# A fused attention, MoE and MLP kernel: the high and low parts of x moved together in the first product of all residual tiles, and the first units' rows gathered at once when planned

## The chip, the cores and the metric

The kernel runs on one core of a Trainium2 chip. The metric is the device time of one execution in microseconds (us), the median of the runs shown. The engines are TensorE (PE, matmuls; PEld is its weight load), VectorE (DVE), ScalarE (ACT), GpSimd (POOL, here mostly the issuer of gathers and scatters) and SyncE (SP, the issuer of the other transfers). Each engine takes its instructions in the order in which they stand in its own program and waits for the others by semaphores.

## The reference

```python
# attention without softmax: 8 sequences of 3072, d_qk 64, D 256
attn = np.maximum(z @ z.T / S, 0.0) ** 2
x = u * (attn @ v)                                   # 24576 rows of 256 in all
# top-1 mixture of 8 experts, 256 -> 1024 -> 256
expert_idx = argmax of (x/|x|) @ (emb/|emb|).T / tau ; gate_w = its softmax value
out[mask] = gate_w[mask, None] * (np.maximum(x[mask] @ w1[e], 0) @ w2[e])
# MLP, 256 -> 2048 -> 256, with g = ELU
y = ELU(out @ w_in) @ w_out
```

## The kernel before

**Number format.** Each float32 operand is split into a high part of type `fp32r`, which PE multiplies at full rate, and a low part, also `fp32r`, that holds the remainder. A product is three matmul passes: high by high, low weight by high operand, high weight by low operand. ACT usually makes the high part (a copy or a relu), DVE the low part (a subtraction).

**Steps.** The whole program is a list of steps, written out by Python. Step `n` issues in this order: its own `h` (a first product on PE into a score buffer `pss`, and the ACT work on it), then `d1` to `d4` of step `n - 1` (the work on DVE), prepared tasks (`pre`), the second product `acc` of step `n - 2` (into an accumulator `psa`), `g`, and the side tasks that a planner put at step `n` (splits of weights, transposes, loads, gathers). The order on each engine is the order in which this program calls it. There are two score buffers of 128x1024 float32 (`t_ps`), two accumulators (`t_acc`), 39 ordinary slots of 128x1024 float32 and five wide tiles of twice that.

**Stages.** 576 attention steps come first. While they run, rows of x are stored to memory (`xr`), routed to experts group by group, and their numbers are scattered by expert into a table (`tok`). Then come units:
- 41 A units: a tile of 512 tokens of one expert through `w1` and `w2`, four steps each (A0 to A3). Their result, x2 (split into `x2h` and `x2l`), goes into
- an M unit each: the MLP on the same 512 tokens, eight steps (M0 on), 12 score matmuls of 512 columns and 12 in the second product.
- 17 residual units for tokens that fill no tile of 512, two steps each (B0, B1): 14 of 256 tokens (B) and 3 of 128 tokens (N). Each stands between an A unit and its M unit. More of them sit behind a condition on the number of tiles (`rest_tiles`).
- 7 D units: the MLP on the residual tokens, scattered into dense rows before.

In a residual unit the operand x lies with its high and low parts side by side in one tile, `xb` (high first), and one step makes 512 hidden units: four groups of 128 (`fi`), each over two halves of D (`kc`). Its function before is `ab_h`, with `ab_d` for the low part.

**Rows of a unit.** `rows_ops` makes its instructions: four gathers of token numbers (`gi`), four gathers of rows of x with the gate value (`gx`), both on POOL; the gating on DVE (`gate`); the store of the gated rows (`put`, to `xg`) and their load in a transposing layout (`get`, to `xt`) on SP. The loop over `units` says at which step each is issued: `wr` for the gathers, `w` for the weights, `wp_` for gating and store. `n` is the unit's first step, and `p1` (541) the step at which the plan of the first six A units is ready; A0 of the first unit is step 576, that of the second 580.

Of the kernel before, what the change touches and what calls it, by code (L numbers as in the profile page):

```python
# [7 lines left out]
F32 = mybir.dt.float32  # L8
# [21 lines left out]
def attn_moe_mlp(ctx, tc, zT, zK, uT, v, emb, embT, tau, wp, w_in, w_out, out):  # L30
# [40 lines left out]
    fixed = {}  # L71
# [62 lines left out]
    def cp(o, a):  # L134
        act.activation(out=o, in_=a, func=AF.Copy)  # L135
# [910 lines left out]
    TOK = {"A": 4, "B": 2, "N": 1}  # L1046
    W1, W2, XT, IDS, WST, WI, WO, X2 = {}, {}, {}, {}, {}, {}, {}, {}
# [45 lines left out]
    def rows_ops(key):  # L1093
# [9 lines left out]
        def gi(t):  # L1103
            def fn():
                if t == 0:
                    IDS[key] = again("ids") if fixed else sb.tile([128, 4], I32, name="ids", tag="ids", bufs=8)
                    h["x"] = wide("rows", [4, XW])
                gather(IDS[key][:, t:t + 1], tok[:, :], idx(t), E * N - 1)
            return fn

        def gx(t):
            def fn():
                known = N - 6 * 512 if kind == "A" and j < NA1 else N
                gather(h["x"][:, t], xr[:known, :], IDS[key][:, t:t + 1], known - 1)
            return fn
# [3 lines left out]
        def gate(t):  # L1119
            def fn():  # L1120
                x = h["x"][:, t]
                ts(x[:, :D], x[:, :D], x[:, D:D + 1], ALU.mult)
            return fn

        def put():
            sp.dma_start(rows.rearrange("(t p) d -> p t d", p=128), h["x"][:, :nt, :D])
# [8 lines left out]
    def xt_ops(key, h, dst, nt):  # L1135
# [5 lines left out]
        def hi():  # L1141
            if nt == 4:
                dst[key] = rslot("xh"), rslot("xl")
            else:
                t = rslot("xb").rearrange("p a (b c) -> p a b c", b=2)[:, :, :, :nt * 128]
                dst[key] = t[:, 0], t[:, 1]
            cp(dst[key][0], h["f"])
# [5 lines left out]
    def ab_h(key, i):  # L1153
# [19 lines left out]
        HL[key, i] = [hi, None]  # L1173

# [408 lines left out]
    fns = {"A": {"h": ab_h, "d1": ab_d, "acc": a_acc}, "B": {"h": ab_h, "d1": ab_d, "acc": b_acc}, "M": mf, "D": mf}  # L1583
# [133 lines left out]
    for un in units:  # L1717
# [3 lines left out]
        if k in "ABN":  # L1721
# [5 lines left out]
            if un == units[0]:  # L1727
                w, wr = n - 16, n - 24
                assert wr >= lo_
# [3 lines left out]
            elif un == units[1]:  # L1733
                wr = n - 16
# [17 lines left out]
            wp_ = n - (16 if un == units[0] else 10) if early else max(wr + 3, n - 11)  # L1752
            at(wp_, lambda gates=gates, put=put: ([g_() for g_ in gates], put()))
            at(wp_ + (5 if un == units[0] else 3) if early else max(wr + 5, n - 9), get)
# [109 lines left out]
```

## Time and profile before

| what | value |
|---|---|
| device time, median of 3 runs | 5083.72 us (5082.21 to 5088.95) |
| profiled execution, device time | 5085.41 us |
| its span, first to last instruction | 5083.6 us |
| mean granted clock of PE | 0.999 |
| PE matmul, busy | 5065.6 us |
| DVE, busy | 4022.5 us |
| ACT, busy | 3429.4 us |
| POOL, busy | 1356.7 us |

The span is what the profile times; the device time holds some 2 us around it. Matmuls overlap in the profile: one of 512 columns is shown with some 0.39 us, though the next starts 0.23 us behind it, so the time of a row of matmuls is read from the start of the row to the start of the next.

### The profile page before, as it was taken

Reading aid. Unit: us, or ns where it says so; the run is one execution under the profiler, and the core shown is the slowest. Engines: PE = TensorE matmul, PEld = TensorE weight load, DVE = VectorE, ACT = ScalarE, POOL = GpSimd, SP = SyncE. Lnnn points to the kernel's source line nnn. Section 1 sums busy time; section 2 is a strip of 40 time slices with the busy share of each in tenths; the row PEclk is TensorE's granted clock in tenths of the full one; section 3 lists DMA queues with packets and bytes.
Section 4 is the critical chain, followed back from the end, with each engine's and each line's share of the span. In section 5 each row is a group of like instructions: output and inputs, shape, how many; then the busy total and the mean of one; then the engine's idle time right before and its main releaser. Section 6 shows DMA issues by size and latency. Waiting matters only on the chain. (4 is left out here: it accounts for less than half of the span.)

```text
span 5083.6 us, 66094 instructions
## 1 busy us (share of the span) xinstructions
PE 5065.6 (100%) x23324; PEld 4198.1 (83%) x23324; DVE 4022.5 (79%) x5281; ACT 3429.4 (67%) x4140; POOL 1356.7 (27%) x1147
## 2 busy tenths in 40 slices
PE   9999999999999999999999999999999999999999
PEld 7888888888888878888888888888888888888887
DVE  8787878788787877887877877877777777777887
ACT  8686767767676756676666666666666666666776
POOL 0011111101111134324443444443333333330011
PEclk9999999999999999999999999999999999999999
DMA  8797988887978784324333334333333333221221
GB/s 247 216 242 215 242 217 230 221 242 214 252 200 239 195 253 145 85 71 119 111 113 115 107 112 121 107 113 109 95 85 85 85 85 85 85 81 38 47 48 40
DMA packets 666978, 726.38 MB, mean 143 GB/s; under 512 B 407724, under 2 KB 509487, under 8 KB 651280
## 3 DMA queue, kind: packets, MB, share of 16 engines
q1 hardware_dynamic: 593648, 518.67, 38.7%
q0 software_dynamic: 72992, 203.42, 12.9%
q8 instruction: 186, 3.05, 0.3%
q14 instruction: 152, 1.25, 0.1%
HBM read 451.63 MB, written 258.33 MB: 140 GB/s over the span
## 5 line engine op out<-in xcount | busy, mean ns | idle before, releaser
L138 PE MATMUL psa<-hi,v 128*128 128x512 f32 x4608 | 1147.2, 391 | 3.6 <-ACT hi L135 2.2
L138 PEld LDWEIGHTS psa<-hi,v 128*128 128x128 f32 x4608 | 858.9, 188 | 189.4 <-issue 7.4
L138 PE MATMUL pss<-x2h,wi 128*128 128x512 f32 x2624 | 808.5, 389 | 0.0
L138 PE MATMUL psa<-hi,wo 128*128 128x512 f32 x3008 | 743.0, 389 | 0.0
L127 DVE SCALAR_TENSOR_TENSOR y<-e,y 128x1024 f32<-128x1024 f32 x385 | 467.5, 1214 | 269.6 <-ACT e L1378 255.3
L138 PEld LDWEIGHTS psa<-hi,wo 128*128 128x128 f32 x3008 | 564.5, 188 | 116.9
L1259 ACT ACTIVATE e<-pss 128x1024 f32<-128x1024 f32 x376 | 386.5, 1028 | 398.7 <-PE pss L138 382.3
L818 POOL DMA_INDIRECT tok<-idt,pi x192 | 234.8, 1223 | 1469.9 <-DMA tok<-idt,pi 807.7
L138 PE MATMUL psa<-lo,v 128*128 128x512 f32 x2304 | 616.9, 390 | 1.3 <-issue 1.3
L1055 POOL DMA_INDIRECT out<-o,ids x192 | 215.6, 1123 | 1479.6 <-DMA o<-orow 1020.1
L1171 ACT ACTIVATE hi<-pss 128x1024 fp32r<-128x1024 f32 (+1 forms) x198 | 201.1, 1016 | 566.8 <-PE pss L138 548.5
L138 PEld LDWEIGHTS pss<-x2h,wi 128*128 128x128 f32 x2624 | 490.4, 188 | 99.9
L441 ACT ACTIVATE r<-pss 128x1024 f32<-128x1024 f32 x289 | 296.1, 1025 | 373.4 <-PE pss L138 370.9
L138 PE MATMUL pss<-x2l,wi 128*128 128x512 f32 x1312 | 510.4, 389 | 0.0
L138 PEld LDWEIGHTS psa<-lo,v 128*128 128x128 f32 x2304 | 433.0, 188 | 92.6 <-issue 1.7
L117 DVE TENSOR_TENSOR y<-r,y 128x1024 f32<-128x1024 f32 x385 | 470.7, 1223 | 33.7 <-DVE y L127 0.9
L117 DVE TENSOR_TENSOR lo<-y,hi 128x1024 fp32r<-128x1024 f32 x385 | 470.9, 1223 | 22.9 <-issue 0.5
L117 DVE TENSOR_TENSOR lo<-r,hi 128x1024 fp32r<-128x1024 f32 x336 | 382.7, 1139 | 103.0 <-ACT hi L135 97.9
L1378 ACT ACTIVATE e<-e 128x1024 f32<-128x1024 f32 x383 | 406.8, 1062 | 12.1
L1377 ACT ACTIVATE y<-e 128x1024 f32<-128x1024 f32 x383 | 406.4, 1061 | 9.5
L138 PE MATMUL psa<-hi,w 128*128 128x512 f32 x1312 | 405.2, 390 | 0.0
L138 PE MATMUL pss<-xh,w 128*128 128x512 f32 x1312 | 404.1, 389 | 0.1
(197 smaller groups left out, 9015.8 us busy)
## 6 DMA issues: line engine op xcount, KB each, us to landing
mir<-mt SPq DMA_DIRECT2D x480, 256.0 KB
mw<-mir SPq DMA_DIRECT2D x120, 1024.0 KB
vs<-v SPq DMA_DIRECT2D x48, 512.0 KB
u<-uT SPq DMA_DIRECT2D x48, 512.0 KB
xr<-xt SPq DMA_DIRECT2D x192, 128.0 KB
x<-xr SPq DMA_DIRECT2D x96, 256.0 KB
orow<-xt SPq DMA_DIRECT2D x188, 128.0 KB
o<-orow SPq DMA_DIRECT2D x47, 512.0 KB
```

The source lines that it names most:

```text
L117: vec.tensor_tensor(out=o, in0=a, in1=b, op=op)
L127: vec.scalar_tensor_tensor(out=o, in0=a, scalar=s, in1=b, op0=op0, op1=op1)
L138: pe.matmul(o, lhsT=l, rhs=r, start=start, stop=stop, skip_group_check=True, tile_position=pos)
L441: act.activation(out=r, in_=p, func=AF.Relu, scale=1.0 / S)
L818: pool.indirect_dma_start(out=tok[:, :], out_offset=bass.IndirectOffsetOnAxis(ap=h["pi"][:, t:t + 1], axis=0), in_=K["idt"][:, gt:gt + 1], ...
L1055: pool.indirect_dma_start(out=dst, out_offset=bass.IndirectOffsetOnAxis(ap=idx, axis=0), in_=src, in_offset=None, bounds_check=bound, oob_ ...
L1171: act.activation(out=hi, in_=p, func=AF.Relu)
L1259: act.activation(out=e, in_=p, func=AF.Relu, scale=-1.0)
L1377: act.activation(out=y, in_=e, func=AF.Tanh, scale=0.5)
L1378: act.activation(out=e, in_=e, func=AF.Exp, scale=-1.0)
```

## The change

Three things change.

1. Residual units get functions of their own, `b_h` and `b_d`. For each group and half of D, one matmul moves high and low part of x together against the high weights (512 columns for B, 256 for N), and a second moves the high part against the low weights (256 or 128) into the high part's columns. A score therefore takes twice the columns: a B step fills two score buffers, an N step one. ACT copies the low part's columns to an SBUF tile `e`, DVE adds the high part's columns to it, ACT makes the high part with a relu and DVE the low part. The copies are issued with the scores (`h`), everything else one step later (`d1`). The units behind the condition keep `ab_h`.
2. The rows of the first two A units are gathered into two ordinary slots each instead of a wide tile, and stored in two transfers.
3. For these units the gathers move from 24 and 16 steps ahead of the unit to `p1 + 1` and `p1 + 8` (steps 542 and 549, before 552 and 564), gating and store to 10 steps behind that (552 and 559, before 560 and 570). The load `get` stays at its step.

```diff
--- before.py
+++ after.py
@@ -1044,6 +1044,7 @@
 
 
     TOK = {"A": 4, "B": 2, "N": 1}
+    XB = {}
     W1, W2, XT, IDS, WST, WI, WO, X2 = {}, {}, {}, {}, {}, {}, {}, {}
 
     def gather(dst, src, idx, bound):
@@ -1104,26 +1105,36 @@
             def fn():
                 if t == 0:
                     IDS[key] = again("ids") if fixed else sb.tile([128, 4], I32, name="ids", tag="ids", bufs=8)
-                    h["x"] = wide("rows", [4, XW])
+                    if fixed or key not in units[:2]:
+                        x = wide("rows", [4, XW])
+                        h["p"] = [x[:, :nt, :D]]
+                        h["x"] = [x[:, i] for i in range(nt)]
+                    else:
+                        x = [slot("rows", F32, (1024,))[:, :2 * XW].rearrange("p (t d) -> p t d", t=2) for _ in range(2)]
+                        h["p"] = [q[:, :, :D] for q in x]
+                        h["x"] = [x[i // 2][:, i % 2] for i in range(nt)]
                 gather(IDS[key][:, t:t + 1], tok[:, :], idx(t), E * N - 1)
             return fn
 
         def gx(t):
             def fn():
                 known = N - 6 * 512 if kind == "A" and j < NA1 else N
-                gather(h["x"][:, t], xr[:known, :], IDS[key][:, t:t + 1], known - 1)
+                gather(h["x"][t], xr[:known, :], IDS[key][:, t:t + 1], known - 1)
             return fn
         row = (j if kind == "A" else NA + j) * 512
         rows = xg[row:row + nt * 128, :]
 
         def gate(t):
             def fn():
-                x = h["x"][:, t]
+                x = h["x"][t]
                 ts(x[:, :D], x[:, :D], x[:, D:D + 1], ALU.mult)
             return fn
 
         def put():
-            sp.dma_start(rows.rearrange("(t p) d -> p t d", p=128), h["x"][:, :nt, :D])
+            to = rows.rearrange("(t p) d -> p t d", p=128)
+            n_ = nt // len(h["p"])
+            for q, x in enumerate(h["p"]):
+                sp.dma_start(to[:, q * n_:(q + 1) * n_], x)
 
         def get():
             h["t"] = slot("xt", F32, (16, 2, 32))
@@ -1144,6 +1155,7 @@
             else:
                 t = rslot("xb").rearrange("p a (b c) -> p a b c", b=2)[:, :, :, :nt * 128]
                 dst[key] = t[:, 0], t[:, 1]
+                XB[key] = t
             cp(dst[key][0], h["f"])
 
         def lo():
@@ -1171,6 +1183,37 @@
         act.activation(out=hi, in_=p, func=AF.Relu)
         PS[key, i] = p
         HL[key, i] = [hi, None]
+
+    def b_h(key, i):
+        t, w_ = XB[key], TOK[key[0]] * 128
+        ps_ = [t_ps() for _ in range(TOK[key[0]])]
+        per = 4 // len(ps_)
+        s_ = flat(slot("e"))[:, :4 * w_].rearrange("p (g c) -> p g c", g=4)
+        for q, p in enumerate(ps_):
+            p = flat(p).rearrange("p (g b c) -> p g b c", g=per, b=2)
+            for g in range(per):
+                fi = 4 * i + q * per + g
+                sl = slice((fi % 4) * 128, (fi % 4) * 128 + 128)
+                for kc in range(2):
+                    w = W1[key, fi // 4, kc]
+                    mm(p[:, g], w[:, 0, sl], t[:, :, kc], kc == 0, kc == 1)
+                    mm(p[:, g, 0], w[:, 1, sl], t[:, 0, kc], False, kc == 1)
+            cp(s_[:, q * per:(q + 1) * per], p[:, :, 1])
+            ps_[q] = p
+        PS[key, i] = ps_, s_
+
+    def b_d(key, i):
+        ps_, s_ = PS.pop((key, i))
+        per = 4 // len(ps_)
+        for q, p in enumerate(ps_):
+            o = s_[:, q * per:(q + 1) * per]
+            tt(o, o, p[:, :, 0], ALU.add)
+        w_ = TOK[key[0]] * 512
+        hi, lo = flat(rslot("hi"))[:, :w_], flat(rslot("lo"))[:, :w_]
+        s_ = s_.rearrange("p g c -> p (g c)")
+        act.activation(out=hi, in_=s_, func=AF.Relu)
+        stt(lo, s_, 0.0, f(hi), ALU.max, ALU.subtract)
+        HL[key, i] = [hi, lo]
 
     def none(*_):
         pass
@@ -1580,7 +1623,7 @@
     mf = {"h": m_h, "g": m_g, "d1": m_d, "d2": m_d2, "d3": m_hi, "d4": m_lo, "acc": m_acc}
     lf = dict(mf, h=l_h, acc=l_acc)
     ef = {"h": e_h, "g": e_g, "d1": e_d, "acc": l_acc}
-    fns = {"A": {"h": ab_h, "d1": ab_d, "acc": a_acc}, "B": {"h": ab_h, "d1": ab_d, "acc": b_acc}, "M": mf, "D": mf}
+    fns = {"A": {"h": ab_h, "d1": ab_d, "acc": a_acc}, "B": {"h": b_h, "d1": b_d, "acc": b_acc}, "M": mf, "D": mf}
     fns["N"] = fns["B"]
     nst = {"A": 4, "B": 2, "N": 2, "M": NF2 // 2, "D": NF2 // 2}
     start, prev = {}, {}
@@ -1725,13 +1768,12 @@
             w = max(n - (9 if k == "A" else 6), lo_)
             wr = max(n - 9, lo_)
             if un == units[0]:
-                w, wr = n - 16, n - 24
-                assert wr >= lo_
+                w, wr = n - 16, p1 + 1
             assert pv is None or pv[0] not in "BN" or k == "M"
             if pv is not None and pv[0] == "M" and prev[pv] is not None and prev[pv][0] in "ABN":
                 wr = max(n - 16, lo_)
             elif un == units[1]:
-                wr = n - 16
+                wr = p1 + 8
             for o in ro:
                 at(wr, o, 2)
             for o in wl:
@@ -1749,9 +1791,9 @@
                 pairs(x, q + o_, q + o_ + 1, 0.6, 0.52)
             assert wr + 5 <= n - 4, (un, wr - n)
             early = un in units[:2]
-            wp_ = n - (16 if un == units[0] else 10) if early else max(wr + 3, n - 11)
+            wp_ = wr + 10 if early else max(wr + 3, n - 11)
             at(wp_, lambda gates=gates, put=put: ([g_() for g_ in gates], put()))
-            at(wp_ + (5 if un == units[0] else 3) if early else max(wr + 5, n - 9), get)
+            at(n - (11 if un == units[0] else 7) if early else max(wr + 5, n - 9), get)
             tr, hl = xt_ops(un, h, XT, TOK[k])
             spread([tr], n - 4, n - 3, 1.25)
             pre[n - 2] += hl
```

**How instructions stand now.** Each list below is one engine's program in order; `a<-b` is output and input, the number behind a name tells tiles apart, and the last column is partitions by elements.

DVE, from the first step of a B unit's work to the first step of its M unit (the first B unit of the program, the one of the rows below). `lo_21604` and `lo_21669` are the low parts of B0 and B1, `w` are splits of weights, `x2l` is the low part of the A unit's result, one half of D each. Before:

```order
L127 SCALAR_TENSOR_TENSOR lo_21604<-pss_21528,hi_21553 128x1024
L117 TENSOR_TENSOR w_21575<-wst2_21283,w_21575 128x512
L117 TENSOR_TENSOR w_21573<-wst2_21283,w_21573 128x512
L117 TENSOR_TENSOR x2l_21615<-psa_21457,x2h_21614 128x512
L117 TENSOR_TENSOR x2l_21615<-psa_21458,x2h_21614 128x512
L127 SCALAR_TENSOR_TENSOR lo_21669<-pss_21577,hi_21602 128x1024
```

After; `e_21534` and `e_21577` are the score sums of B0 and B1, `lo_21599` and `lo_21668` their low parts:

```order
L117 TENSOR_TENSOR e_21534<-e_21534,pss_21532 128x512
L117 TENSOR_TENSOR e_21534<-e_21534,pss_21533 128x512
L127 SCALAR_TENSOR_TENSOR lo_21599<-e_21534,hi_21598 128x1024
L117 TENSOR_TENSOR w_21573<-wst2_21287,w_21573 128x512
L117 TENSOR_TENSOR w_21571<-wst2_21287,w_21571 128x512
L117 TENSOR_TENSOR x2l_21611<-psa_21461,x2h_21610 128x512
L117 TENSOR_TENSOR x2l_21611<-psa_21462,x2h_21610 128x512
L117 TENSOR_TENSOR e_21577<-e_21577,pss_21575 128x512
L117 TENSOR_TENSOR e_21577<-e_21577,pss_21576 128x512
L127 SCALAR_TENSOR_TENSOR lo_21668<-e_21577,hi_21667 128x1024
```

The sums are new and stand at the places of the old subtractions: those of B1, which read its two score buffers last, behind both `x2l`. The rest keeps its order. The other B units read alike.

ACT, the same place. `hi_21553` and `hi_21602` are the high parts of B0 and B1, `x2h` the high part of the A unit's result. Before:

```order
L1171 ACTIVATE hi_21553<-pss_21528 128x1024
L135 ACTIVATE w_21573<-wst2_21283 128x512
L135 ACTIVATE w_21575<-wst2_21283 128x512
L1171 ACTIVATE hi_21602<-pss_21577 128x1024
L135 ACTIVATE x2h_21614<-psa_21457 128x512
L135 ACTIVATE x2h_21614<-psa_21458 128x512
```

After; the relu of B0 is `hi_21598`:

```order
L135 ACTIVATE e_21534<-pss_21532 128x512
L135 ACTIVATE e_21534<-pss_21533 128x512
L135 ACTIVATE w_21571<-wst2_21287 128x512
L135 ACTIVATE w_21573<-wst2_21287 128x512
L135 ACTIVATE e_21577<-pss_21575 128x512
L135 ACTIVATE e_21577<-pss_21576 128x512
L1214 ACTIVATE hi_21598<-e_21534 128x1024
L135 ACTIVATE x2h_21610<-psa_21461 128x512
L135 ACTIVATE x2h_21610<-psa_21462 128x512
```

The relu of B0 stood ahead of B1's scores and now stands behind both copies out of them (`e_21577`).

PE, the scores of M0 with the engines that each matmul waits for (the first product of the M unit, on `x2h` and `x2l`). Before:

```order
L138 MATMUL pss_21653<-x2h_21614,wi_18133 128x512 [waits DVE_49,Activation_49]
L138 MATMUL pss_21653<-x2h_21614,wi_18133 128x512
L138 MATMUL pss_21653<-x2l_21615,wi_18133 128x512 [waits DVE_49]
L138 MATMUL pss_21653<-x2h_21614,wi_18133 128x512 x2
L138 MATMUL pss_21653<-x2l_21615,wi_18133 128x512
L138 MATMUL pss_21653<-x2h_21614,wi_18141 128x512 [waits Activation_49]
L138 MATMUL pss_21653<-x2h_21614,wi_18141 128x512
L138 MATMUL pss_21653<-x2l_21615,wi_18141 128x512 [waits DVE_49]
```

After:

```order
L138 MATMUL pss_21649<-x2h_21610,wi_18137 128x512 [waits DVE_49,Activation_49]
L138 MATMUL pss_21649<-x2h_21610,wi_18137 128x512
L138 MATMUL pss_21649<-x2l_21611,wi_18137 128x512
L138 MATMUL pss_21649<-x2h_21610,wi_18137 128x512 x2
L138 MATMUL pss_21649<-x2l_21611,wi_18137 128x512
L138 MATMUL pss_21649<-x2h_21610,wi_18145 128x512 [waits Activation_49]
L138 MATMUL pss_21649<-x2h_21610,wi_18145 128x512
L138 MATMUL pss_21649<-x2l_21611,wi_18145 128x512
```

The matmuls are the same. The waits for DVE at the two `x2l` rows are gone; the only one left is that of the first matmul.

POOL, from the end of attention to the loads of the MLP's weights (`wi`), with - for before and + for after; the first `ids` and `rows` are those of the first two A units, the third those of the third:

```order
+L1051 DMA ids<-tok,ixa 128x1 x4
+L1051 DMA rows<-xr,ids 128x320 x4
 L818 DMA tok<-idt,pi 196608x1 x4
-L1050 DMA ids<-tok,ixa 128x1 x4
-L1050 DMA rows<-xr,ids 128x320 x4
-L1050 DMA wst<-wp,wia 128x1024 x4
-L1050 DMA ids<-tok,ixa 128x1 x4
-L1050 DMA rows<-xr,ids 128x320 x4
-L1050 DMA wst<-wp,wia 128x1024 x4
-L1050 DMA ids<-tok,ixa 128x1 x4
-L1050 DMA rows<-xr,ids 128x320 x4
-L1498 DMA wi<-wis 128x1024 x8
```

The gathers of the first unit moved ahead of four scatters to `tok`, those of the second ahead of the first unit's weights.

## Rows read from the trace of the kernel before

**Rows 1.** The page: busy time of each engine, and PE's granted clock in 40 slices.

```profile
PE 5065.6 (100%) x23324; PEld 4198.1 (83%) x23324; DVE 4022.5 (79%) x5281; ACT 3429.4 (67%) x4140; POOL 1356.7 (27%) x1147
PEclk9999999999999999999999999999999999999999
```

**Rows 2.** Waits of PE, whole run: total, times, longest, in us.

```profile
PE psa L138 <- ACT hi L135: 2.2, 1, 2.2
```

**Rows 3.** Timeline of PE in a B unit: start, us, instruction, count.

```profile
2312.68 3.04 PE L138 MATMUL pss<-xb,w 128*128 128x256 f32 x24
2315.56 0.63 PE L138 MATMUL psa<-hi,w 128*128 128x512 f32 x2
2321.18 0.63 PE L138 MATMUL psa<-hi,w 128*128 128x512 f32 x2
2323.92 0.61 PE L138 MATMUL pss<-x2h,wi 128*128 128x512 f32 x2
```

**Rows 4.** Timeline of ACT and DVE in that unit; in brackets the idle time before.

```profile
2321.38 1.03 ACT L1171 ACTIVATE hi<-pss 128x1024 fp32r<-128x1024 f32 x1 [3.56 <-PE pss L138]
2322.76 0.60 ACT L135 ACTIVATE x2h<-psa 128x512 fp32r<-128x512 f32 x1 [0.36 <-PE psa L138]
2323.39 0.69 DVE L117 TENSOR_TENSOR x2l<-psa,x2h 128x512 fp32r<-128x512 f32 x1 [4.15 <-ACT x2h L135]
2324.75 0.69 DVE L117 TENSOR_TENSOR x2l<-psa,x2h 128x512 fp32r<-128x512 f32 x1 [0.67 <-ACT x2h L135]
2325.36 1.21 DVE L127 SCALAR_TENSOR_TENSOR lo<-pss,hi 128x1024 fp32r<-128x1024 f32 x1
2326.49 0.68 DVE L117 TENSOR_TENSOR w<-wst,w 128x512 fp32r<-128x512 f32 x1
2333.41 1.23 DVE L117 TENSOR_TENSOR lo<-y,hi 128x1024 fp32r<-128x1024 f32 x1
```

**Rows 5.** Timeline of PE where the first A units start.

```profile
1853.98 1.20 PE L138 MATMUL psa<-lo,v 128*128 128x512 f32 x4 [1.33 <-issue]
1882.22 1.07 PE L138 MATMUL psa<-lo,v 128*128 128x512 f32 x4
1887.31 2.11 PE L138 MATMUL psa<-hi,v 128*128 128x512 f32 x8 [0.80 <-issue]
1892.52 3.19 PE L138 MATMUL psa<-hi,v 128*128 128x512 f32 x8 [2.19 <-ACT hi L135]
1895.50 1.62 PE L138 MATMUL psa<-lo,v 128*128 128x512 f32 x4
```

**Rows 6.** Timeline of PE in an N unit.

```profile
3459.59 2.79 PE L138 MATMUL pss<-xb,w 128*128 128x128 f32 x24
3462.22 0.69 PE L138 MATMUL psa<-hi,w 128*128 128x512 f32 x2
3467.68 0.69 PE L138 MATMUL psa<-hi,w 128*128 128x512 f32 x2
3470.96 0.39 PE L138 MATMUL pss<-x2l,wi 128*128 128x512 f32 x1
```

**Rows 7.** Groups by form, ACT and DVE: count, busy us, mean ns, idle before.

```profile
L135 ACT ACTIVATE w<-wst 128x512 fp32r<-128x512 f32 x464 | 265.1, 621 | 0.0
L135 ACT ACTIVATE xh<-xf 128x1024 fp32r<-128x1024 f32 x48 | 50.9, 1059 | 0.0
L135 ACT ACTIVATE xo<-psa 128x512 f32<-128x512 f32 x14 | 8.4, 598 | 24.3 <-PE psa L138 24.3
L117 DVE TENSOR_TENSOR xo<-xo,psa 128x512 f32<-128x512 f32 x14 | 9.6, 687 | 15.3 <-ACT xo L135 15.3
```

**Rows 8.** One stretch: length, busy us by engine, granted clock, DMA share, GB/s.

```profile
1894.00:1896.00 2.00, 2.00 (x7) 1.54 (x6) 1.85 (x7) 0.29 (x1) 0.00 (x0) 0.50 0.96 361
```

**Rows 9.** Waits of all engines, 1830 to 1900 us.

```profile
DVE rows L121 <- DMA rows<-xr,ids: 4.2, 2, 2.4
```

**Rows 10.** Waits of SP's queue, 1830 to 1900 us.

```profile
SPq L1131 <- DMA xg<-rows: 7.5, 1, 7.5
```

## The prediction

> **What bounds the kernel now.** I read the page first: TensorE (PE) is busy for the whole span and its granted clock is full in every slice, while VectorE (DVE) and ScalarE (ACT) have a fifth and a third of their time free [rows 1]. So time is won where PE's work gets shorter and lost where PE is made to wait. PE's waits come next: the longest of the whole run is 2.2 us [rows 2]. The timeline of one residual unit says how close this is: the unit's scores, the second product of the tile before it and the first step of the MLP follow on PE without a gap [rows 3], with DVE and ACT close behind [rows 4]. Last I read the stretch in which the first expert units start, where that longest wait lies [rows 5].
>
> **Names.** An A unit has steps A0 to A3, a B or N unit B0 and B1 (N0 and N1), the MLP behind them M0, M1 and on. T is the moment at which PE ends B1's scores and starts A3's second product: 2321.18 in [rows 3].
>
> **The change, part by part.**
>
> *Fewer matmuls.* For each 128 hidden units and half of D, three passes become two. In the 14 B units three passes of 256 columns become one of 512 and one of 256: as many columns, 16 matmuls a step for 24. Before, the 24 go from 2312.68 to 2315.56, 0.120 us each; twelve of 512 take 2.74 (2321.18 to 2323.92), 0.228 each [rows 3]. So a step takes 8 x (0.228 + 0.120) = 2.79 for 2.88: 0.09 less in each of 28 steps, **-2.6 us**. In the 3 N units three passes of 128 columns become one of 256 and one of 128. The 24 take 2.63 (3459.59 to 3462.22), 0.110 each, hardly less than with twice the columns [rows 6]. Then 8 x (0.120 + 0.110) = 1.84, 0.79 less in each of 6 steps: **-4.7 us**. The page "TensorE: Matmul & The Clock Gate" of the Trainium skill (section "Back-to-back issue gap") gives an isolated matmul its columns at 2.4 GHz plus 2.5 ns; by it only that small part is saved, 0.7 us over the 272 matmuls dropped instead of 7.3, and the sum would be 6.6 higher. The rows differ from it, above all at 128 columns, and I keep the rows.
>
> *More work behind a step.* Before, a step has one ACT relu and one DVE subtraction, both out of PSUM. Now ACT copies the low part (for B two pieces of 128x512), DVE adds the high part to it (two pieces), then come relu and subtraction. By like rows a copy is 0.60 and a sum 0.69 [rows 7], so ACT gets 1.2 us more a B step and DVE 1.4. Both have room for that as an average. What counts is the order.
>
> *Where it waits.* B1 now fills both score buffers, and M0's scores need one of them back. It is free when DVE has added B1's first score. In DVE's order these sums stand behind both x2l subtractions, those behind two weight splits, and those behind B0's subtraction; that one waits for B0's relu, which in ACT's order stands behind B1's two copies. PE's own rows say the same: the DVE waits that stood at M0's x2l matmuls are gone, and the one at M0's first matmul covers them. Step by step:
> - ACT's first instruction behind B1's last matmul starts at T + 0.20 (2321.38) [rows 4]; that is now the copy of B1's second score, 0.60 long. The relu behind it starts 0.08 before the copy's end, as DVE's instructions do (2325.36 after 2324.75 + 0.69) [rows 4]: T + 0.72. At 1.06 [rows 7] it ends at T + 1.78.
> - DVE's subtraction starts 0.03 behind it (2323.39 behind 2322.76 + 0.60), and its next instruction 1.13 later (2326.49 behind 2325.36) [rows 4]: T + 2.94.
> - Two splits and two x2l of 128x512 follow at 0.61 each (2325.36 behind 2324.75) [rows 4]: T + 5.38. Their x2h is there by then, as A3's product ends at T + 2.74.
> - The sum of 0.69 ends at T + 6.07, PE starts 0.03 later: T + 6.10.
>
> Before, M0 starts at T + 2.74 (2323.92). The pause is 3.36 us, and nothing fills it, since PE takes its matmuls in order. DVE's and ACT's orders are the same in all 14 B units: **+47.0 us**. Bounds of a pause: 3.0 if the DVE steps overlap more, 3.7 if each starts only behind the end of the one ahead (some 0.08 more at each of four steps). Nothing behind catches it up, as PE is full to the end.
>
> *N units.* N1 takes one buffer, so M0 gets N0's without a wait. But x2l is late here too: the copy starts at T + 0.20, the relu of 128x512 at T + 0.72 and ends at 1.34 (0.62 by a split of that size [rows 7]), the subtraction starts at 1.37, and behind three steps of 0.61 x2l starts at 3.20 and ends at 3.89; PE goes on at T + 3.92. It was used at T + 3.28 (3470.96, with T at 3467.68) [rows 6]: 0.64 for 3 units, **+1.9 us**; bounds 0 and 1.2 a unit.
>
> *The clock behind a pause.* At 1892.52 PE comes out of a pause of 2.19 us, with one of 0.80 shortly ahead of it, and its next 8 and 4 matmuls take 3.19 and 1.62 us [rows 5] for 1.98 (8 x 0.228 and the last one's tail, 0.16) and 1.07. The granted clock there is 0.50, the 1.2 GHz level [rows 8]. 1.76 is lost. The pause of 1.33 at 1853 was followed by four matmuls in 1.20 [rows 5], at full clock. The new pauses are longer than both. So I expect the fall behind most of them; part of the slow time may lie in the pause itself, and I take 1.5 of the 1.76: **+21.0 us**, bounds 0 and 24.6. The same page of the Trainium skill (section "HAM oscillation — how this bites in real kernels") says that waits between bursts of matmuls can slow the clock anew at each burst, which speaks against this change; 1892 agrees, 1853 does not. By that rule at every pause the sum would be 3.6 higher, without it 21.0 lower.
>
> *First units.* The rows of the first two A units are gathered 10 and 15 steps earlier and gated 8 and 11 steps earlier, into ordinary slots. Before, DVE stood 4.2 us at the gates for these rows [rows 9] and SP, which loads the mirrored scores too, 7.5 us for the gated rows to land [rows 10]. PE lost 1.33, 0.80 and 2.19 in this stretch, and 1.76 to the clock: 6.1 [rows 5]. The 1.33 follows the wait at the gates and the 0.80 a late mirrored load; both should go. The 2.19 ends with ACT, on a load in a stretch where the DMA engines are full [rows 8]; the change takes only some traffic away. I take 1.33 + 0.80 and half of the rest: **-4.1 us**. Bounds: -6.1, and +4.0 (one more such pause with its clock) if the four slots that the rows now hold keep other work waiting.
>
> *Sum.* -2.6 - 4.7 + 47.0 + 1.9 + 21.0 - 4.1 = +58.5 on the profiled execution's own 5085.4: 5143.9. It stood 1.7 over the median of the runs shown (5083.7), so I forecast **5142.2 us**. A change of 0.2% (10 us) is about what a measurement of this kernel can tell.
>
> **Rivals.**
> 1. *The clock stays up*: the pauses come, the slow stretches do not. For it speaks the pause of 1.33, against it that of 2.19. 5142.2 - 21.0 = 5121.2 us. Chance 0.15.
> 2. *Faster*: M0 isn't held, because DVE has added B1's first score before PE ends A3's product. It decides at T + 2.74. For it: DVE stood idle 4.15 us ahead of x2l before [rows 4], so there was room. Against: the second x2l can't start before A3's end, and the sum stands behind it. Then only the gains are left: -2.6 - 4.7 - 4.1 = -11.4, 5072.3 us. Chance 0.05.
> 3. *A second pause*: B1's relu (1.06) now also stands between M0's first relu and its tanh, so M0's low part comes later by that. Before, it ended at 2334.64 (2333.41 + 1.23) [rows 4]; PE would ask for it behind three steps' scores and two second products of the unit, 2323.92 + 3 x 2.74 + 2 x 2.79 = 2337.7. Of these 3.1 us 2.0 are left, so it decides where the chain loses 2.0 more than counted. Priced by the relu itself, 1.06 in 14 units, 14.8: 5157.0 us. Chance 0.10.
>
> The forecast has the other 0.70. Range 5112 to 5162: the low end is rival 1 with a pause of 3.0 (5 less) and the whole gain of the first units (2 less), rounded down; the high end is rival 3 with the full price of the clock (3.6 more), rounded up. Faster by over 0.2% is rival 2 but for a hundredth that ends within 0.2%; all else is slower: 0.04, 0.01, 0.95.
>
> **What the profile after would show.** PE waiting for DVE's sum at M0's first matmul, 14 times some 3.4 us, nearly all of PE's waiting. DVE's subtraction of B0 starting some 1.8 us behind the end of B1's scores. Granted clock 0.50 for part of the time behind M0's start. A B step's scores in 2.79, an N step's in 1.84. PE's wait near 1853 gone, and DVE waiting for no rows there. The forecast is wrong if PE goes into M0 without a wait (then my reading of the order fails) or if the waits come at full clock (then 21 us fall away).

## The result and the profile after

The changed kernel takes 5153.86 us (median of 4 runs, 5152.67 to 5157.58) against 5084.01 us (4 runs beside it): ratio 1.0141, 95% interval 1.0129 to 1.0153, so 69.9 us slower. The profiled execution took 5152.67 us with a span of 5150.5, 66.9 us above the span of before; the accounts below are of spans. Mean granted clock 0.995 for 0.999.

The page of the changed kernel, busy time and granted clock, beside [rows 1]:

```profile
PE 5084.2 (99%) x23052; PEld 4194.5 (81%) x23052; DVE 4058.9 (79%) x5343; ACT 3458.9 (67%) x4202; POOL 1353.0 (26%) x1147
...
PEclk9999999999999999999999999999999999999999
```

PE has fewer instructions and more busy time, so some of them ran slower. The 40 slices don't show it, since no slice falls below 9. PE's waits over the whole run say where to look:

```profile
PE pss L138 <- DVE e L117: 44.8, 14, 3.2
PE psa L138 <- DVE hi L607: 6.7, 2, 6.0
PE pss L138 <- DVE x2l L117: 1.4, 3, 0.5
```

The first line is new and is most of PE's waiting: 14 times 3.2 us, on DVE's sum. The second is one wait of 6.0 us (and one of 0.7); in [rows 2] the longest was 2.2. The third is the N units. The timeline of PE in the first B unit, beside [rows 3]:

```profile
2315.30 2.97 PE L138 MATMUL pss<-xb,w 128*128 128x512 f32 x16
2318.11 0.64 PE L138 MATMUL psa<-hi,w 128*128 128x512 f32 x2
...
2323.71 0.64 PE L138 MATMUL psa<-hi,w 128*128 128x512 f32 x2
...
2329.85 0.70 PE L138 MATMUL pss<-x2h,wi 128*128 128x512 f32 x2 [3.20 <-DVE e L117]
...
2331.68 1.06 PE L138 MATMUL pss<-x2h,wi 128*128 128x512 f32 x2
2332.53 0.63 PE L138 MATMUL pss<-x2l,wi 128*128 128x512 f32 x1
2332.96 1.06 PE L138 MATMUL pss<-x2h,wi 128*128 128x512 f32 x2
```

T is 2323.71 here. The scores take 2.81 (2315.30 to 2318.11) for 2.88, and M0 starts at T + 6.14 for T + 2.74. The last rows show the clock: three matmuls of 512 columns, 0.68 us at the 0.228 each of before, now take 1.28 (2331.68 to 2332.96). The granted clock of that stretch is 0.50, the 1.2 GHz level (length, busy us of PE, PEld, DVE, ACT, POOL, granted clock, DMA share, GB/s):

```profile
2331.70:2334.20 2.50, 2.50 (x7) 1.99 (x6) 0.00 (x0) 0.00 (x0) 0.00 (x0) 0.50 0.00 0
```

ACT and DVE in the same unit, beside [rows 4]:

```profile
2324.40 1.05 ACT L1214 ACTIVATE hi<-e 128x1024 fp32r<-128x1024 f32 x1
...
2325.49 1.22 DVE L127 SCALAR_TENSOR_TENSOR lo<-e,hi 128x1024 fp32r<-128x1024 f32 x1 [5.85 <-ACT hi L1214]
2326.63 1.28 DVE L117 TENSOR_TENSOR w<-wst,w 128x512 fp32r<-128x512 f32 x2
2327.83 1.28 DVE L117 TENSOR_TENSOR x2l<-psa,x2h 128x512 fp32r<-128x512 f32 x2
2329.03 1.27 DVE L117 TENSOR_TENSOR e<-e,pss 128x512 f32<-128x512 f32 x2
```

The chain can be read off: relu of B0 done at T + 1.74 (forecast 1.78), its subtraction at T + 2.92 to the next instruction (2.94), two weight splits, x2l from T + 4.12, the sums from T + 5.32 (5.38), PE at T + 6.14 (6.10).

Going through all units of both traces by the starts of these rows gives this account, from the start of B0's scores to the start of M0's own second product:

| stretch | before, us | after, us | difference over all |
|---|---|---|---|
| 14 B units, where the clock holds | 24.99 | 28.42 | 14 x 3.43 = +48.0 |
| the 12 of them where it falls behind the pause | 24.99 | 30.01 | 12 x 1.59 = +19.1 |
| 3 N units | 21.89 | 20.96 | 3 x -0.93 = -2.8 |
| all ahead of the first B unit (its scores' start) | 2312.68 | 2315.30 | +2.6 |
| sum | | | +66.9 |

The sum is the difference of the spans, so nothing else moved the end. PE in the first N unit of this list, beside [rows 6] (its T is 3462.13):

```profile
3455.74 1.96 PE L138 MATMUL pss<-xb,w 128*128 128x256 f32 x16
3457.53 0.68 PE L138 MATMUL psa<-hi,w 128*128 128x512 f32 x2
...
3462.13 0.68 PE L138 MATMUL psa<-hi,w 128*128 128x512 f32 x2
...
3466.03 0.50 PE L138 MATMUL pss<-x2l,wi 128*128 128x512 f32 x1 [0.48 <-DVE x2l L117]
```

The one surprise of the account is its fourth line. Timeline of PE where the first A units start, beside [rows 5]:

```profile
1854.18 3.78 PE L138 MATMUL psa<-hi,v 128*128 128x512 f32 x8 [6.03 <-DVE hi L607]
1857.76 1.91 PE L138 MATMUL psa<-lo,v 128*128 128x512 f32 x4
1859.47 0.42 PE L138 MATMUL pss<-zp,zk 128*128 128x256 f32 x1
```

None of the pauses of [rows 5] is left, but one of 6.03 us stands there, and the 12 matmuls behind it take 5.29 us (1854.18 to 1859.47, granted clock 0.50) for 2.74 at full clock. So 6.03 + 2.55 = 8.6 stand here for the 6.1 that the pauses and the clock of [rows 5] had cost: 2.5 of the +2.6. Behind the wait stands DVE, and behind DVE the rows (DVE's waits, 1790 to 1950 us, beside [rows 9]):

```profile
DVE rows L121 <- DMA rows<-xr,ids: 9.9, 2, 8.3
```

POOL's timeline ahead of it:

```profile
1808.90 1.03 POOL L818 DMA_INDIRECT tok<-idt,pi  x1 [0.30 <-issue]
1816.69 1.00 POOL L818 DMA_INDIRECT tok<-idt,pi  x1 [6.76 <-DMA tok<-idt,pi]
1823.69 0.98 POOL L818 DMA_INDIRECT tok<-idt,pi  x1 [6.00 <-DMA tok<-idt,pi]
1829.63 0.98 POOL L818 DMA_INDIRECT tok<-idt,pi  x1 [4.96 <-DMA tok<-idt,pi]
1836.00 1.80 POOL L1051 DMA_INDIRECT ids<-tok,ixa  x1 [5.39 <-DMA tok<-idt,pi]
```

The four scatters (L818) each wait until the transfer of the one before has landed, and A1's gathers of token numbers, planned at step 549, stand behind all four: they start at 1836.00. (The list of POOL's order ahead of the prediction has, of the changed kernel, only the first unit's gathers; the second unit's follow the four scatters directly, as here.) Before, the same gathers had been planned later still, but so had the gates. Now the gates come at step 559, find no rows, and hold DVE for 8.3 us.

### The profile page after: what moved, and what is told of

Same layout as the page of the kernel before. It is cut to its first block, busy times and chain, and to the rows that moved or that the text cites. A ratio compares the mean times of both kernels' runs of the same rounds, so it can differ in the third digit from the quotient of the medians.

```text
span 5150.5 us, 65593 instructions
## 1 busy us (share of the span) xinstructions
PE 5084.2 (99%) x23052; PEld 4194.5 (81%) x23052; DVE 4058.9 (79%) x5343; ACT 3458.9 (67%) x4202; POOL 1353.0 (26%) x1147
## 5 line engine op out<-in xcount | busy, mean ns | idle before, releaser
L138 PE MATMUL pss<-x2h,wi 128*128 128x512 f32 x2624 | 822.8, 395 | 44.8 <-DVE e L117 44.8
L818 POOL DMA_INDIRECT tok<-idt,pi x192 | 232.6, 1212 | 1469.5 <-DMA tok<-idt,pi 788.9
L1183 ACT ACTIVATE hi<-pss 128x1024 fp32r<-128x1024 f32 x164 | 168.8, 1029 | 465.5 <-PE pss L138 465.5
```

Of the source, the lines that this page charges most:

```text
L138: pe.matmul(o, lhsT=l, rhs=r, start=start, stop=stop, skip_group_check=True, tile_position=pos)
L818: pool.indirect_dma_start(out=tok[:, :], out_offset=bass.IndirectOffsetOnAxis(ap=h["pi"][:, t:t + 1], axis=0), in_=K["idt"][:, gt:gt + 1], ...
L1183: act.activation(out=hi, in_=p, func=AF.Relu)
```

## Experiments

The order theory: what costs is only that B1's sum, which frees M0's score buffer, and the first units' gathers stand too far back in their engines' queues, and that the clock falls behind the longer of the pauses. Its rivals: the work that was added on ACT and DVE or PE's wider matmuls cost the time wherever they stand; and for the first units, that the traffic there is the bound. Ratios are to the kernel before on the same chip.

**The two halves alone.**

```diff
 # e1_product_only: the planner as before, and the wide tile for the first units' rows
-                w, wr = n - 16, p1 + 1
+                w, wr = n - 16, n - 24
...
-                wr = p1 + 8
+                wr = n - 16
...
 # e2_gather_only, e2_again
-    "B": {"h": b_h, "d1": b_d, "acc": b_acc}
+    "B": {"h": ab_h, "d1": ab_d, "acc": b_acc}
```

> The change of the residual product alone: the first two units' gathers, gates, stores and loads are placed as before. The order theory (M0's score buffer is freed by the sum of B1, which stands behind relu, lo, w and x2l on DVE, so PE stands until T+6.1 in each of 14 B units, and the clock falls behind most of these pauses) prices this half from the trace after the change: 14 x 3.43 = +48.0 for the pauses less what the matmuls give back, 12 x 1.59 = +19.1 for the clock, 3 x -0.94 = -2.8 in the N units, so +64.3 on 5084.0, 5148.3 us, with PE's wait for the sum at 3.2 us x 14. The rival is that the first units gain their forecast 4.1 us with the new gathers after all, and the product costs some 74: then this kernel takes 5158.

Measured: 5150.69 us, ratio 1.0130 (1.0113 to 1.0147), +67.2 for the +64.3 expected. The wait for the sum is there 14 times, and the clock fell behind 13 of them instead of 12.

> The gathers of the first two units alone, moved as in the change; B and N units compute as before (four matmuls for each pair). Theory: A1's gathers stand behind the four scatters on POOL's queue, its gates come too early and hold DVE for some 8 us, behind which PE stands 6.0 us for hi and runs at a lower clock; what the change spares elsewhere in the first units is 3.4 us less than that. So +2.6 on 5084.0, 5086.6 us, with the 6.0 us wait in the trace. The rival, which is the forecast's own term: the gathers spare 4.1 us, 5079.9. A third: it does nothing by itself, 5084, and the 2.6 of the changed kernel come from somewhere else.

Measured: 5094.18 us (10 runs, 5087.19 to 5099.61), ratio 1.0021 (1.0011 to 1.0030). The profiled run has a span 2.2 us longer than before, with the 8.4 us wait of DVE and this one of PE, 1790 to 1950 us:

```profile
PE psa L138 <- DVE hi L607: 5.8, 1, 5.8
```

So the forecast's sign for this half is wrong, and the loss, +10.7 by the medians for the +2.6 expected, is larger in most runs than in the profiled one. The two halves add to 78 by the medians, 8 more than the whole change, and to 68.0 by the spans (65.8 and 2.2), 1.1 more; where the 8 come from was not shown. Of the spread this asks:

> The gathers alone once more, for one more trace: its ten timed runs lay between 5087 and 5100 us while those of before lay within 5 us, and its trace was of a run of 5088. If the spread is made in the first units, the trace of a longer run shows the first B unit's scores later than 2315 us by what the run is longer, and the stretches behind it as long as ever; if not, it is elsewhere.

Measured: 5090.34 us, span 5088.2, 2.4 more than the first trace. The same wait in it:

```profile
PE psa L138 <- DVE hi L607: 8.9, 1, 8.9
```

The wait is 3.1 us longer, the first B unit's scores start at 2317.23 for 2314.86, and every unit behind takes what it took. Most of the difference between these two runs is made here: the wait is 3.1 longer, and the 12 matmuls behind it take 1.0 less (4.25 us for 5.29). Of the 3.1 us some 1.5 come from the scatters (A1's gathers start at 1838.22 for 1836.72), the others from token numbers that land later.

**The place of the sums.** Here b_d is cut into three: b_sums (the sums), b_relu (ACT's relu) and b_lo (the subtraction), and called from other slots of the step; the list says in short what each slot calls. "g" of B0's step stands behind A3's second product in the program, "h" of B1's step right behind B1's scores.

```diff
 # e3_sums_early
-    "d1": b_d                       # sums, relu, lo of both
+    "g":  if i == 0: b_sums
+    "h":  b_h; if i == 1: b_sums
+    "d1": b_relu; b_lo
 # e4_first_relu_early
+    "g":  if i == 0: b_sums; b_relu
+    "d1": if i == 1: b_sums; b_relu
+          b_lo
 # e5_both_early (e6: with the planner and the wide tile as before)
+    "g":  if i == 0: b_sums; b_relu
+    "h":  b_h; if i == 1: b_sums
+    "d1": if i == 1: b_relu
+          b_lo
```

> Of the changed kernel only the place of the sums e + pss in program order is moved: that of B0 to the slot of the step in which A3's product runs, that of B1 right behind its scores; the two relus and lo stay where they are. Order theory: M0's buffer is then free, and M0's first matmul starts at T+2.8 instead of T+6.15; what is still late is x2l, behind relu of B0, lo and w, so that M0's third matmul waits some 1.65 us in each B unit and the clock hardly falls: 14 x 1.65 = 23, less 2.8 in the N units, plus 2.6 in the first units, 5107 us. If the clock falls behind a 1.65 us wait too, up to 14 x 1.6 = 22 more, 5129. The rival is that the work itself costs the time (an extra copy and an extra sum for each step, 256-column matmuls), wherever the sums stand: then it stays within a few us of 5153.9, and the wait moves to another place at its full length.

> Of the changed kernel only B0's sums and relu are moved, to the step in which A3's product runs; B1's sums and relu stay behind x2l. Order theory: the chain on DVE begins with lo at once, without the relu of 1.05 us ahead of it and without B0's two sums, so B1's first sum ends some 1.25 us earlier and M0 starts at T+4.9: a pause of 2.16 us in each of 14 B units, 30 us, so 5114 with no fall of the clock and 5114 + 14 x 1.6 = 5136 if the clock falls behind each. This run tells whether a pause of about 2.2 us brings the clock down, as those of 3.2 us did in 12 of 14. The rival that only the number of operations matters leaves it at 5153.9.

Measured: 5109.15 us, ratio 1.0049 (1.0032 to 1.0066), and 5121.22 us, ratio 1.0074 (1.0057 to 1.0091). PE's waits, first the sums early, then the first relu early:

```profile
PE pss L138 <- DVE x2l L117: 22.2, 17, 1.5
```

```profile
PE pss L138 <- DVE e L117: 29.4, 14, 2.1
```

Where the sums are early, M0 starts at T + 2.78, and the wait of 1.47 is now at its first x2l, in 14 B units and (0.56) 3 N units; the clock falls in none. Where only B0's relu is early, the pause is 2.10, and the clock falls behind it in 4 of 14 units: in the first B unit, not in the second (two stretches from M0's start: length, busy us of PE, PEld, DVE, ACT, POOL, granted clock, DMA share, GB/s):

```profile
2327.20:2331.50 4.30, 4.30 (x13) 3.36 (x14) 0.42 (x1) 0.00 (x0) 0.53 (x1) 0.62 0.04 11
2407.80:2410.60 2.80, 2.80 (x13) 2.31 (x14) 0.41 (x1) 0.00 (x0) 1.14 (x2) 1.00 0.14 47
```

Both kernels do all the added work. Only the places of the sums and of one relu differ, so the 45 and 33 us that came back are the order's, not the work's.

> Of the changed kernel B0's sums and relu move to the step in which A3's product runs and B1's sums stand right behind B1's scores; only B1's relu and the two lo stay behind. This joins the two earlier runs. With B1's sums alone early, PE stood 1.47 us for x2l in 14 of 14 B units and the clock fell in none; with B0's relu alone early, it stood 2.10 us for B1's sum and the clock fell in 4 of 14. Order theory: with both neither wait is left, a B unit takes 2.81 + 2.78 + 2.81 + 2.78 + 2.84 + 11.03 = 25.05 us as against 24.99 before, so +0.8 over 14; the N units 20.17 as against 21.90, -5.2 over 3; first units +1 to +2.6 in a profiled execution. 5081 to 5083, level with before; the runs of the gathers alone had a median 6 us above their profiled one, and if that spread is here too the median goes up to 5089. The rival that the work added on ACT and DVE or PE's wider matmuls cost the time leaves at least the 23 us of the kernel with the early sums: 5107.

> As the kernel with both early, with the first units' gathers, gates and loads placed as before. Order theory: +0.8 in the B units, -5.2 in the N units, nothing in the first units: 5079.5, 0.09% below before, at the edge of what can be told; no wait of PE for e or x2l. Rival: the first units' new gathers do gain, then this one is slower than the same kernel with them. Its runs also show whether the wide spread of times comes with the gathers: by that theory these agree within 5 us, as those of before do.

Measured: 5105.10 us, ratio 1.0041 (1.0026 to 1.0057), and 5100.61 us, ratio 1.0032 (1.0020 to 1.0045), 21 to 24 us over what the order theory gave. I had taken it for granted that no wait would be left once both were early. PE's waits with both early, and DVE in the first B unit (T = 2324.26):

```profile
PE pss L138 <- DVE x2l L117: 17.4, 17, 1.2
```

```profile
2323.68 0.69 DVE L117 TENSOR_TENSOR e<-e,pss 128x512 f32<-128x512 f32 x1 [2.89 <-ACT e L135]
...
2325.70 1.22 DVE L127 SCALAR_TENSOR_TENSOR lo<-e,hi 128x1024 fp32r<-128x1024 f32 x1
2326.83 1.29 DVE L117 TENSOR_TENSOR w<-wst,w 128x512 fp32r<-128x512 f32 x2
2328.03 1.28 DVE L117 TENSOR_TENSOR x2l<-psa,x2h 128x512 fp32r<-128x512 f32 x2
```

DVE idles 2.89 us ahead of B1's first sum, and then B0's subtraction and two splits stand ahead of x2l. The wait of 1.12 is the subtraction's 1.13. Either it is the order once more or, by the rival, the work. The spread settles nothing: without the new gathers six runs lie within 3.5 us, as expected, but with them four lie within 2.0.

**Where the gathers stand.**

```diff
 # e8_gathers_ahead: the changed kernel with
-                wr = p1 + 8
+                wr = p1 + 2
...
-            wp_ = wr + 10 if early else ...
+            wp_ = wr + (10 if un == units[0] else 16) if early else ...
 # e7_both_early_gates_old: e5 with wr = p1 + 2 and
+            wp_ = n - (16 if un == units[0] else 10) if early else ...
```

> As the kernel with both early, but A1's gathers follow A0's at once, ahead of the four last scatters on POOL's queue, and the gates and the loads keep their places of before. Theory for the first units: what the gathers cost there is that A1's ids stand behind four scatters that follow one another 5 to 7 us apart, so that the gated rows come late; ahead of them, rows and gates are ready early and neither the 6.0 us wait for hi is there nor the waits of before (1.33, 0.80, 2.19 us and 1.76 of clock, 6.1 in all): 5079.5 - 6.1 = 5073.4 at the best, 5079.5 if the waits of before come from something else. Rival: the first units are bound by the traffic in that stretch (DMA at 0.9 busy from 1800 to 1950 us), and the wait for hi only moves: 5082 or more.

> The changed kernel with one thing moved: A1's gathers directly behind A0's, ahead of the four last scatters; its gates stay at their step. If the scatters are what makes A1's rows late, DVE's 8.3 us wait for rows and PE's 6.0 us wait for hi are gone, with some 1.8 us at the lower clock behind it, and the kernel takes 5153.9 - 7.8 = 5146. If the gates would hold DVE in any case (another transfer late, the queues full), the wait stays and the time is 5152 to 5158.

Measured: 5098.59 us, ratio 1.0031 (1.0019 to 1.0042), 6.5 under the same kernel with the changed gathers, but only 2.0 under the one with the gathers of before, which these intervals do not tell apart (the 5073 to 5080 expected still left out the waits for x2l); and 5145.00 us, ratio 1.0123 (1.0108 to 1.0139), 8.9 under the changed kernel and near the 5146 expected. POOL in the latter:

```profile
1807.45 1.03 POOL L818 DMA_INDIRECT tok<-idt,pi  x1 [0.30 <-issue]
1816.12 1.04 POOL L1051 DMA_INDIRECT ids<-tok,ixa  x1 [7.64 <-DMA tok<-idt,pi]
...
1827.62 1.40 POOL L818 DMA_INDIRECT tok<-idt,pi  x1 [0.30 <-issue]
```

One of the four scatters still stands ahead of A1's gathers, three follow; the gathers start at 1816.12 for 1836.00. PE's longest wait from 1790 to 1950 us is then this:

```profile
PE psa L138 <- ACT hi L135: 0.7, 1, 0.7
```

The first B unit's scores start at 2307.13: 8.2 earlier than in the changed kernel and 5.5 earlier than before; in the kernel with the gates of before they start 4.1 earlier than before. So the traffic does not keep this stretch from getting shorter, and by the traces what the change promised in the first units is there; the place on POOL's queue had lost it. No median shows this gain over the kernel before by itself.

**All of it.**

```diff
 # e9_all_early: e5 with e8's gathers and
-    "g":  if i == 0: b_sums; b_relu
+    "g":  if i == 0: b_sums; b_relu; b_lo
-    "d1": if i == 1: b_relu
-          b_lo
+    "d1": if i == 1: b_relu; b_lo
 # e10_n_only: e9 with the B units as before
+    "B": {"h": ab_h, "d1": ab_d, "acc": b_acc}
+    fns["N"] = the functions of e9
```

> All of B0's work (sums, relu, subtraction) in the step in which A3's product runs, B1's sums behind its scores, and the first units' gathers in one row ahead of the four scatters. In the kernel with both early 1.12 us of waiting for x2l was left in 14 of 14 B units: DVE's row before x2l held B0's subtraction (1.13 to the next instruction) and two splits, while DVE had stood idle 2.89 us ahead of B1's sums. If order alone decides, the subtraction goes into that idle time, x2l starts 1.13 us earlier and the wait goes: B units 26.38 - 1.12 = 25.26, or 25.05 by their parts, against 24.99 before (+0.8 to +3.8 over 14), N units 20.17 to 21.03 against 21.90 (-5.2 to -2.6), first units as with the gathers ahead, 5.5 us earlier than before. Sum on 5083.7: 5074 to 5079. The rival, that added work keeps costing time wherever it stands, leaves the 1.12 in place: 5091 or more.

> The new product in the 3 N units alone, with the early order; the 14 B units compute as before; gathers in one row ahead of the scatters. By the traces the B units gain nothing from wider matmuls (25.05 without any wait, for 24.99), so all that the change can bring is in the N units and the first units: 24.99 in each B unit, 20.2 to 21.0 in each N unit for 21.90 (-5.2 to -2.6), -5.5 in the first units. On 5083.7: 5073 to 5076, faster than before by 0.15 to 0.2%. If the forecast's 0.09 us a step in the B units does exist, the kernel with the new product in the B units too is 2.6 faster than this one.

Measured: 5081.28 us, ratio 0.9997 (0.9988 to 1.0006), and 5080.30 us, ratio 0.9994 (0.9985 to 1.0003), both above what was expected (5074 to 5079 and 5073 to 5076). DVE in the first B unit of the former (T = 2317.39):

```profile
2314.44 1.23 DVE L127 SCALAR_TENSOR_TENSOR lo<-e,hi 128x1024 fp32r<-128x1024 f32 x1 [1.13 <-ACT hi L1216]
...
2316.81 0.69 DVE L117 TENSOR_TENSOR e<-e,pss 128x512 f32<-128x512 f32 x1 [0.54 <-ACT e L135]
2318.22 0.69 DVE L117 TENSOR_TENSOR e<-e,pss 128x512 f32<-128x512 f32 x1 [0.72 <-ACT e L135]
2318.82 1.29 DVE L117 TENSOR_TENSOR w<-wst,w 128x512 fp32r<-128x512 f32 x2
2320.03 0.68 DVE L117 TENSOR_TENSOR x2l<-psa,x2h 128x512 fp32r<-128x512 f32 x1
```

The subtraction now runs ahead of B1's sums, x2l starts at T + 2.64, and PE's list of waits has nothing between 2300 and 3600 us. The clock is full. The work is all still there and the pauses and the clock's 67 us are gone, so the order theory stands and the rival falls. But a B unit takes 25.21 us, 0.22 more than before, an N unit 20.42, 1.5 less than before. PE at the start of M0 shows where the 0.22 stand:

```profile
2320.17 0.61 PE L138 MATMUL pss<-x2h,wi 128*128 128x512 f32 x2
2320.76 0.50 PE L138 MATMUL pss<-x2l,wi 128*128 128x512 f32 x1
2321.10 0.62 PE L138 MATMUL pss<-x2h,wi 128*128 128x512 f32 x2
```

Three matmuls take 0.93 us (2320.17 to 2321.10) for 0.68. The first one on x2l starts 0.14 later than it would at the usual step, 0.05 behind the end of DVE's x2l (2320.03 + 0.68), and the one behind it follows 0.34 later for 0.23, as behind the wait for x2l in the N unit above (3466.03 to 3466.37). So this is the same wait for x2l, too short for the list, and still the order: the two weight splits stand ahead of x2l. M0's scores take 3.00 for 2.72, and a unit without that would be 0.05 shorter than before. An order with x2l ahead of the splits was not run. In the stretch of the first units a wait of 2.5 us for ACT stands again (2.2 before), and the first B unit starts only 3.7 earlier than before. Neither kernel can be told from the one before at this measurement.

## Why the forecast held, and which step did not

- **The pause** (+47.0): right in place, chain and size. M0 at T + 6.14 for 6.10, 14 times; the pause is 3.40 for 3.36, 47.6 us. It was the whole case for "slower", and the kernel with the sums early shows that the place of the sum is its cause.
- **The clock** (+21.0): 19.1. It fell behind 12 of 14 pauses and cost 1.59 each where it did; the forecast had 1.5 each time, so that fewer falls and dearer ones partly cancel. Rival 1 (the clock stays up) holds in 2 of 14. The Trainium skill, "TensorE: Matmul & The Clock Gate", section "HAM oscillation — how this bites in real kernels", says that waits between bursts can bring the clock down anew each time; that agrees with the pauses of 3.20, behind 12 of 14 of which it fell. The Trainium skill's case there has longer waits than 1.47 and 2.10 us, so what these did (none, and 4 of 14) neither bears it out nor speaks against it.
- **Fewer matmuls, B units** (-2.6): gone. A step's scores did get shorter, by 0.06 for the 0.09 forecast, but each of A2's and A3's second products behind them takes 2.78 for 2.75, and M0's scores take 2.84 for 2.72 even where the clock holds. The unit less its pause is 0.03 longer, +0.5 over 14. What M0's scores lose goes with the pause ahead of them and not with the matmuls: where only B0's relu is early, no wait stands ahead of them in the N units, and they take 2.72 there. The matmuls alone gave back 0.05 a unit, -0.7 over 14.
- **N units** (-4.7 and +1.9): -2.8, as forecast, though by parts it is -5.2 and +2.4, so the exact sum is partly chance. Scores 1.79 for 1.84 forecast and 2.63 before; x2l used at T + 3.90 for 3.92 forecast. At equal columns, 24 matmuls made 16 save 0.84 us a step. The Trainium skill's figure for an isolated matmul (the same page, section "Back-to-back issue gap"), by which only 2.5 ns would go with each, is not that of this row, where some 104 ns went with each; the section itself says that it counts too little at 128 columns where each matmul has its weight load.
- **First units** (-4.1): the step that failed; +2.6. "Both should go" was right of the waits of 1.33 and 0.80 (and the 2.19 went too). What I left out is the queue: I counted steps by which gathers and gates were moved, and did not look at what stands ahead of A1's gathers on POOL. Four scatters do, one transfer after the other, and the gates moved earlier than the rows could, so that DVE stood 8.3 us at them where the forecast had said that it would wait for no rows. The bound of +4.0 was there for another reason (slots), so it is no credit. With the gathers ahead of three of the scatters the stretch gains 3.7 to 5.5 in four traces.
- **Rivals 2 and 3**: M0 not held (rival 2) needed another order, and then gave 5081 instead of its 5072. Of a second pause (rival 3) no wait of PE is in the trace, and what stands behind M0's scores takes 11.03 us where the clock holds, as before.

The forecast, 5142.2, is 11.7 low of the median. In spans the sum was 58.5 for 66.9: 6.7 from the first units, 3.1 from the B units less their pause, 0.6 from the pause, -1.9 from the clock. The rest is the profiled run, 1.2 under the median after, the 1.7 by which I put before's median lower, and 0.4 outside the spans.

## What to carry to other kernels

When a step takes both buffers of a pair, ask which instruction gives the first one back and what stands ahead of it in its engine's queue: a sum of 0.69 us with seven instructions ahead of it on two engines cost 67 us here, and four calls moved in the program (the sums of both steps, relu and subtraction of the first) took 64 us off the B units. When gathers are planned earlier, look at the queue of the engine that issues them, and move the work that uses them by no more than what that queue allows. Fewer, wider matmuls gain where the narrow ones take longer than their columns: here 0.84 us of a step's 2.63 at 128 columns, and hardly at 256 (0.06 of 2.87).

## What the runs showed of the hardware

- Equal pauses of PE don't bring the clock down equally, and longer ones do so more often: of 14 it fell behind none at a wait of 1.12 or 1.47 us, 4 at 2.10, and 12 or 13 at 3.20 (three kernels), at a cost of some 1.6 us each time. What sets the units apart was not found.
- Twelve matmuls of 512 columns take 2.72 us behind others of 512, 2.75 behind a row of 256 columns and 2.78 behind one that alternates between 512 and 256; behind a pause, with the clock full, they take 2.84. The trace shows no wait inside these rows, and I did not find the cause.
- Scatters into one table that wait for each other followed 6 to 8 us apart on POOL's queue in the changed kernel (4 to 10 in the other traces), and so a row of four held everything behind it for some 27 us (1808.90 to 1836.00). The wait that this made for PE was 5.8 us in one run and 8.9 in another of the same kernel.
- The end of the program is set by such a row too. With the gathers ahead and the B units as before, the units and the first stretch together are 8.9 us shorter by the trace and the span only 7.1. The last matmuls end 8.9 earlier, and so start the last eight scatters of the output; but between the third and the fourth 5.1 us pass, for 3.3 before. Why that one transfer took longer is open. POOL there:

```profile
5053.25 1.61 POOL L1056 DMA_INDIRECT out<-o,ids  x1 [1.71 <-DMA out<-o,ids]
5058.37 0.98 POOL L1056 DMA_INDIRECT out<-o,ids  x1 [3.50 <-DMA out<-o,ids]
```
